# The opening of a fused attention and expert kernel, written out operation by operation

## The chip, the cores and the metric

The kernel runs on one core of one Trainium2 chip. The metric is the device time of one launch, in microseconds (us), as the median over several runs. Before the change it is 823.41 us (three runs, 822.85 to 825.19).

## The reference, cut to what matters

Attention over a band of keys for 4 batches, 8 heads, 576 positions and 64 dimensions, and then a mixture of four experts for every one of the 2304 positions:

```
scores = q @ k.T / sqrt(64)             # heads 0-3: the last 32 keys
scores = where(mask, scores, -1e9)      # heads 4-7: every 4th of the last 128 keys
attn   = exp(scores - max) / (sum + 1e-9)
x      = attn @ v                       # 2304 x 512 after a transpose of the heads
p      = domain_probs / (sum + 1e-9)
out    = sum over e of p[:, e] * (relu(x @ w1[e]) @ w2[e])   # w1[e] 512 x 1024, w2[e] 1024 x 512
```

All data are float32. The products of the experts are made from a high and a low part of each operand, three matmuls each, in a scheme with fewer block products (the names B11, B21, T1, S1 and so on are blocks and sums of blocks).

## The kernel before, in words

**Attention in steps.** A group is two heads of one batch and 192 positions; a step (`steps[m]`) is two groups. Each step goes through the same operations: `s_qk` (24 small matmuls on TensorE into two PSUM banks, tile `sc`, L300), `s_max` (six VectorE instructions that add the mask and take the row's extreme value, tiles `sm` and `nm`, L314), `s_sub` (GpSimd, L328), `s_exp` (ScalarE, L335), `s_sum` (VectorE: a sum, an added epsilon and a reciprocal, L345 to L351), `s_norm` (GpSimd, L358), `s_tr` (three transposes on TensorE into `pt`, L369, and ScalarE's copy into `pts`, L373), `s_av` (24 small matmuls into two banks `po`, L389) and `s_out` (two copies from `po` into the rows of x, tile `xr`, by ScalarE, L413, or VectorE, L411). The tiles `sc`, `pt` and `po` share a ring of four PSUM banks.

**Rounds.** The loop at L921 goes through rounds n = 0, 1, 2 and so on. In each it emits, in the order of a table (`first`, `ahead`, `turned`, `apart`, L419 ff.), the operations of several steps: the scores of step n, the sums of step n-1, the transposes of step n-2 and the product with v of step n-3. Between rounds `dummies` (L820, tile `wt`) put matmuls without use on TensorE. What one engine executes is then in exactly the order in which the program wrote it; engines wait for each other by semaphores.

**From attention to experts.** Steps 0 to 4 give the first 384 rows of x that the first expert product needs: block B11 from steps 0 to 2, block B21 from steps 3 and 4. `START` is 7, the round after which these are done. `x_part` splits a block into a high part (`xh_B`, ScalarE, L130) and a low part (`xl_B`, VectorE for one half and GpSimd for the other, L127); `w1_split` does the same with w1 (tiles `g1h`, `g1l`, and `hh12`, `hl12` for block A21), `w2_late` with w2 (`w2h`, `w2l`). `experts` emits the products: `m1x` and `m1y` (L475), then `m` (L579), whose results VectorE adds into `acc` (L583, L588). From then on attention steps are woven between expert products.

**Loads.** SyncE (queue SP) issues almost every load, in the order of the list `loads` (L879); ScalarE issues k of step 0 and the masks. A load goes out when its condition in `ready` holds, and an item that is not ready holds back what follows. v of a step is two transfers, one to partitions 0 to 63 and one to partitions 64 to 127. The entry `fenced` puts a one-element memset on VectorE ahead of v of steps 2, 3 and 4, and w1 has one too (L108), so that these transfers leave after VectorE has reached that place. w1 of the first unit comes in halves: A11 and A21 first (`("w1", 0)`), A12 and A22 later (`("rest", 0)`). The eight hardware semaphores of the transfers are used in turn, so a transfer also waits until the one eight places before it has landed.

## Time and profile before

| | us |
|---|---|
| median of three runs | 823.41 (822.85 to 825.19) |
| the profiled execution | 823.21 |
| its span, first to last instruction | 821.4 |
| TensorE matmuls busy | 812.7 (99%) |
| VectorE / ScalarE / GpSimd busy | 483.5 (59%) / 314.7 (38%) / 390.3 (48%) |
| first expert product m1x starts | 23.49 |
| its second operand block, from steps 3 and 4 | 27.03 |
| the expert products m (L579) go on after their last wait in the opening | 34.27 |
| granted TensorE clock, mean | 1.00 |

Times in the trace count from the first instruction of the span. The busy share of TensorE is a sum over matmul records and counts dummies as work; what a stretch is limited by is read from the chain of waits, which goes back from the last instruction to what released each step.

### The profile page before, as it was taken

To read this page: it belongs to the slowest core of one execution; us is meant where nothing else is said; L and a number is where in the kernel's file an instruction comes from. 1 tells how busy PE (TensorE), PEld (TensorE's weight loads), DVE (VectorE), ACT (ScalarE), POOL (GpSimd) and SP (SyncE) were. 2 spreads that over 40 slices of the span, in tenths; PEclk is the share of its full clock that TensorE was granted. 3 is DMA by queue.
4 is the path that set the end of the run, shared out by engine and by line. 5 is a ranking of instruction groups with operands and counts; after the bars stand their busy time and mean duration, and the time that the engine had idled before them with its cause. 6 is when DMAs were issued, how large, how long until landed. Compare 5 with 4: busy or idle time off the path is not lost.

```text
span 821.4 us, 15447 instructions
## 1 busy us (share of the span) xinstructions
PE 812.7 (99%) x6162; PEld 720.8 (88%) x6162; DVE 483.5 (59%) x1058; ACT 314.7 (38%) x749; POOL 390.3 (48%) x465
## 2 busy tenths in 40 slices
PE   8999999999999999999999999999999999999998
PEld 5778888888888889889889889889889989989987
DVE  5887557665765777555554554554554554555555
ACT  3554454544455446224223323323323323333321
POOL 4546878786777879334233233233243143153110
PEclk9999999999999999999999999999999999999999
DMA  7764624245211124110010010010010010010003
GB/s 230 230 180 132 193 71 133 83 128 158 91 53 52 52 92 140 35 43 26 26 51 27 26 52 26 26 52 26 27 52 26 26 52 26 27 51 1 1 26 128
DMA packets 46770, 59.15 MB, mean 72 GB/s; under 512 B 2905, under 2 KB 36313, under 8 KB 46699
## 3 DMA queue, kind: packets, MB, share of 16 engines
q1 hardware_dynamic: 46283, 57.75, 22.4%
q8 instruction: 48, 0.79, 0.4%
q10 hardware_dynamic: 416, 0.43, 0.1%
q14 instruction: 23, 0.19, 0.1%
HBM read 53.45 MB, written 4.72 MB: 71 GB/s over the span
## 4 chain that ended last, share of the span: by engine, by line
PE 92%; DVE 4%; DMA 1%; ACT 1%; issue 1%; POOL 0%; SPq 0%; POOLq 0%; DVEq 0%; ACTq 0%
PE m L579 46%; PE m1y L475 24%; PE m1x L475 18%; PE po L389 2%; DMA r<-w 1%; PE sc L300 1%; PE wt L824 1%; PE pt L369 1%; DVE xr L227 1%; DVE acc L588 1%; DVE sm L314 1%; DVE hl L499 0%; DVE su L345 0%; ACT hh L493 0%; DVE su L347 0%
## 5 line engine op out<-in xcount | busy, mean ns | idle before, releaser
L588 DVE SCALAR_TENSOR_TENSOR acc<-m,pn,acc 128x512 f32<-128x512 f32 (+1 forms) x271 | 202.2, 747 | 132.0 <-PE m L579 131.9
L579 PE MATMUL m<-w2h,hh 128*128 128x512 f32 x578 | 227.7, 394 | 0.8 <-DVE acc L588 0.3
L579 PE MATMUL m<-w2l,hh 128*128 128x512 f32 x578 | 225.5, 390 | 0.0
L127 POOL TENSOR_TENSOR g2l<-r,g2h 128x256 fp32r<-128x256 f32 x116 | 85.2, 759 | 235.0 <-PE m L579 212.7
L579 PE MATMUL m<-w2h,hl 128*128 128x512 f32 x578 | 179.0, 390 | 0.0
L493 ACT ACTIVATE hh<-s 128x384 fp32r<-128x384 f32 x92 | 48.3, 526 | 236.3 <-DVE s L516 185.2
L579 PEld LDWEIGHTS m<-w2h,hl 128*128 128x128 f32 x578 | 108.3, 188 | 24.5 <-DVE hl L499 1.0
L579 PEld LDWEIGHTS m<-w2h,hh 128*128 128x128 f32 x578 | 108.5, 188 | 23.2 <-DVE acc L588 2.6
L579 PEld LDWEIGHTS m<-w2l,hh 128*128 128x128 f32 x578 | 108.6, 188 | 19.5
L127 POOL TENSOR_TENSOR g1l<-r,g1h 128x256 fp32r<-128x256 f32 x93 | 70.0, 773 | 65.6 <-ACT g1h L130 65.6
L127 POOL TENSOR_TENSOR w2l<-r,w2h 128x512 fp32r<-128x512 f32 x58 | 75.2, 1315 | 47.1 <-ACT w2h L130 47.1
L535 DVE TENSOR_TENSOR s<-m1y,s 128x384 f32<-128x384 f32 x46 | 25.6, 556 | 93.8 <-PE m1y L475 92.3
L526 ACT ACTIVATE u<-m1y 128x384 f32<-128x384 f32 x46 | 22.6, 492 | 146.0 <-PE m1y L475 146.0
L499 DVE SCALAR_TENSOR_TENSOR hl<-s,hh 128x384 fp32r<-128x384 f32 x92 | 55.3, 601 | 27.7 <-ACT hh L493 27.5
L475 PE MATMUL m1y<-xh_T,g2h 128*128 128x384 f32 x152 | 51.9, 341 | 0.0
L475 PE MATMUL m1y<-xl_T,g2h 128*128 128x384 f32 x152 | 51.2, 337 | 0.0
L475 PE MATMUL m1y<-xh_T,g2l 128*128 128x384 f32 x152 | 51.0, 336 | 0.0
L130 ACT ACTIVATE g2h<-r 128x256 fp32r<-128x256 f32 x120 | 42.2, 407 | 0.8 <-POOL r L168 0.8
L475 PE MATMUL m1x<-xh_B,g2h 128*128 128x384 f32 x124 | 41.7, 337 | 0.0
L475 PE MATMUL m1x<-xl_B,g2h 128*128 128x384 f32 x124 | 41.7, 336 | 0.0
L475 PE MATMUL m1x<-xh_B,g2l 128*128 128x384 f32 x124 | 41.4, 334 | 0.0
L130 ACT ACTIVATE w2h<-r 128x512 fp32r<-128x512 f32 x64 | 38.3, 622 | 4.6 <-DMA r<-w 4.6
(133 smaller groups left out, 1477.2 us busy)
## 6 DMA issues: line engine op xcount, KB each, us to landing
r<-w SPq DMA_DIRECT2D x63, 512.0 KB, 3.3
v_s<-vw SPq DMA_DIRECT2D x48, 192.0 KB, 4.6
k_s<-kT SPq DMA_DIRECT2D x23, 224.0 KB, 4.8
q_s<-qT SPq DMA_DIRECT2D x24, 192.0 KB, 4.7
out<-acc SPq DMA_DIRECT2D x17, 256.0 KB, 2.0
r<-w SPq DMA_DIRECT2D x2, 256.0 KB, 4.3
out<-acc SPq DMA_DIRECT2D x2, 128.0 KB, 1.9
k_s<-kT ACTq DMA_DIRECT2D x1, 224.0 KB, 3.7
```

What stands on the lines that cost most here:

```text
L127: lo_eng.tensor_tensor(out=lo, in0=src, in1=hi.bitcast(F32), op=ALU.subtract)
L130: nc.scalar.activation(out=hi, in_=src, func=AF.Copy)
L227: nc.vector.tensor_tensor(out=quarter(i, d), in0=quarter(i, a), in1=quarter(i, b), op=ALU.subtract)
L300: nc.tensor.matmul(banks[swap][o:o + QB, i * KB:(i + 1) * KB], q_s[h, c0:c0 + QB], k_s[h, c0:c0 + KB], start=True, stop=True, skip_group_c ...
L389: nc.tensor.matmul(po[k][64 * j:64 * j + 64, o:o + QB], v_s[rows, j, 2 * i + half, :], ts_[rows, c:c + QB], start=True, stop=True,)
L475: nc.tensor.matmul(bank, w[:, k], x[:, k], start=(first and k == 0 and i == 0), stop=(last and k == 1 and i == 2), skip_group_check=True,)
L493: nc.scalar.activation(out=hi, in_=src, func=AF.Relu)
L499: nc.vector.scalar_tensor_tensor(out=lo, in0=src, scalar=0.0, in1=hi.bitcast(F32), op0=ALU.max, op1=ALU.subtract)
L526: nc.scalar.activation(out=u2, in_=x, func=AF.Copy)
L535: nc.vector.tensor_tensor(out=s5, in0=x, in1=s5, op=ALU.add)
L579: nc.tensor.matmul(po, h, w[:, d], start=(n == 0 and x == 0), stop=(n == 3))
L588: nc.vector.scalar_tensor_tensor(out=acc[:, d], in0=po, scalar=pn[:, tt, e:e + 1], in1=acc[:, d], op0=ALU.mult, op1=ALU.add,)
```

## The change

The rounds 0 to 7 no longer follow one table. `opening` lists the operations of every round. In it the sums of step n-2 (before: n-1) stand inside the maxima of step n: `s_both` emits the sum, then three of the six maxima, then the epsilon and the other three, then the reciprocal. The product with v of step m comes in round m+4 (before: m+3), and the scores of step 3 come ahead of the first transpose. Steps 3 and 4 get softmax buffers of their own, in tiles that the experts use later (`s1`, `hh21`). The second half of v of steps 0 to 3 is issued by ScalarE at the start, the first half by SyncE; the fences of v of steps 2 to 4 and of w1 go, and the first half of w1 goes out in round 1, ahead of v of step 1. The high parts of A11 and A21 are made in round 3, their low parts held until round 6. The copies out of `po` for steps 2, 3 and 4 are shared, one by ScalarE and one by VectorE (before: both by VectorE for steps 1 and 2, both by ScalarE for the others). Five dummies instead of seven stand between the rounds (1792 columns instead of 2560). After round 7 the program is as before.

```diff
-            if u in (0, 2):
+            if u == 2:
                 nc.vector.memset(raw1[u][:, 0, :1], 0.0)
...
-        def load_v(n, gs, fence):
-            t = ap.tile([128, 2, GB, 64], F32, tag="v", name="v_s", bufs=VB)
+        def load_v(n, gs, fence, halves=range(2), queue=nc.sync):
+            if n not in v_of:
+                v_of[n] = ap.tile([128, 2, GB, 64], F32, tag="v", name="v_s", bufs=VB)
+            t = v_of[n]
             if fence:
                 nc.vector.memset(t[:, 0, 0, :1], 0.0)
-            for k, (b, p, gi) in enumerate(gs):
-                nc.sync.dma_start(
+            for k in halves:
+                b, p, gi = gs[k]
+                queue.dma_start(
                     out=t[KB * k:KB * (k + 1)], in_=vw[b, p][:, :, gi * GB:(gi + 1) * GB, :]
                 )
-            v_of[n] = t
 
         def s_qk(n, gs):
             banks = [pa.tile([128, 512], F32, tag="pa", name="sc") for _ in gs]
...
-        def s_max(n, gs):
+        def max_parts(n, gs):
             banks = st[n]
-            sm = ap.tile([128, 2 * GS, KB], F32, tag="sm", name="sm", bufs=3)
+            if n in (3, 4):
+                sm = fp.tile([128, TH], F32, tag=("s1", "hh21")[n - 3], name="sm")
+                sm = sm.rearrange("q (k c) -> q k c", c=KB)
+            else:
+                sm = ap.tile([128, 2 * GS, KB], F32, tag="sm", name="sm", bufs=3)
             nm = ap.tile([128, 2 * GS], F32, tag="nm", name="nm", bufs=3)
...
-            st[n] = (sm, nm)
+                st[n] = (sm, nm)
+                yield
+
+        def s_max(n, gs):
+            for _ in max_parts(n, gs):
+                pass
 
         def s_sub(n, gs):
             sm, nm = st[n]
...
+            next(beside, 0)
             for su, rc, sm in ops:
                 nc.vector.tensor_tensor(
                     out=su, in0=su, in1=eps.to_broadcast([128, 2 * GS]), op=ALU.add
                 )
+            for _ in beside:
+                pass
             for su, rc, sm in ops:
                 nc.vector.reciprocal(out=rc, in_=su)
 
         def s_sum(n, gs):
             s_sums([(n, gs)])
+
+        def s_both(n, gs):
+
+            s_sums([(n - 2, steps[n - 2])], max_parts(n, gs))
 
         def s_norm(n, gs):
             sm, rc = st[n]
...
-                if 0 < n < 3:
+                if 1 < n < 5 and k:
...
-        ahead = (
-            (s_qk, 0), (s_max, 0), (s_sum, 1), (s_sub, 0), (s_norm, 1), (s_exp, 0),
-            (s_av, 3), (s_tr, 2),
+        stages = (first, apart, then)
+        opening = (
+            ((s_qk, 0), (s_max, 0), (s_sub, 0), (s_exp, 0)),
+            ((s_qk, 1), (s_max, 1), (s_sub, 1), (s_exp, 1)),
+            ((s_qk, 2), (s_both, 2), (s_sub, 2), (s_norm, 0), (s_exp, 2)),
+            ((s_qk, 3), (s_both, 3), (s_sub, 3), (s_norm, 1), (s_tr, 0), (s_exp, 3)),
+            ((s_qk, 4), (s_both, 4), (s_sub, 4), (s_norm, 2), (s_av, 0), (s_tr, 1), (s_exp, 4)),
+            ((s_sum, 3), (s_norm, 3), (s_av, 1), (s_tr, 2)),
+            ((s_sum, 4), (None, 0), (s_norm, 4), (s_tr, 3), (s_av, 2), (s_tr, 4)),
+            ((s_av, 3), (s_av, 4)),
         )
-        turned = ((s_tr, 2), (s_av, 3))
-        stages = (first, apart, then, ahead, turned)
 
         def pairs_of_steps(new, old, begun, loaded):
 
...
         qk_done, av_done = [0], [0]
         shares = []
         ready = {"w2": lambda u: u < 1 or (u - 1, 1) in w2_op and (u < 2 or n >= OPEN)}
-        ready["w1"] = lambda u: n >= (needed[0] + 1, 0, OPEN)[u]
+        ready["w1"] = lambda u: n >= (1, 0, OPEN)[u]
         waits = {
-            needed[0] + 1: needed[0] + 1, needed[1] + 1: OPEN - 2, needed[1] + 2: OPEN,
+            needed[0] + 1: START - 1, needed[1] + 1: OPEN - 2, needed[1] + 2: OPEN,
         }
         ready["qk"] = lambda m: m < qk_done[0] + QKB and n >= waits.get(min(m, needed[1] + 2), 0)
-        fenced = {2: (3, 0), 3: (3, 1), 4: (3, 1), 7: (START + 4, 0), 8: (START + 5, 0)}
+        fenced = {7: (START + 4, 0), 8: (START + 5, 0)}
         ready["v"] = lambda m: (
             m < av_done[0] + VB
             and (m <= needed[1] or m <= qk_done[0] and n >= OPEN)
-            and (n, mid) >= fenced.get(m, (0, 0))
+            and (n, 0) >= fenced.get(m, (0, 0))
         )
 
         def load(what, m):
             if what == "qk":
                 load_qk(steps[m], nc.sync if m else nc.scalar, m in waits)
             elif what == "v":
-                load_v(m, steps[m], m in fenced)
+                load_v(m, steps[m], m in fenced, range(1 if m < VB else 2))
+            elif what == "half":
+                load_v(m, steps[m], False, range(1, 2), nc.scalar)
             elif what == "masks":
                 load_masks()
             elif what == "rest":
...
-            ("qk", 0), ("masks", 0), ("qk", 1), ("qk", 2), ("v", 0), ("qk", 3), ("qk", 4),
-            ("v", 1), ("v", 2), ("v", 3), ("v", 4), ("w1", 0), ("qk", 5), ("rest", 0), ("probs", 0),
+            ("qk", 0), ("masks", 0), ("half", 0), ("half", 1), ("half", 2), ("half", 3),
+            ("qk", 1), ("qk", 2), ("v", 0), ("qk", 3), ("qk", 4), ("w1", 0), ("v", 1), ("v", 2),
+            ("v", 3), ("v", 4), ("rest", 0), ("qk", 5), ("probs", 0),
             ("w2", 0), ("qk", 6), ("w1", 1), ("qk", 7), ("v", 5), ("qk", 8), ("qk", 9),
...
-                flush()
-                holding.clear()
                 due = 0
-            early_order = {4: 3, 5: 3, START - 1: 4}.get(n, START + 1 < n < OPEN - 2)
-            for k, order in enumerate((stages[early_order], stages[2])):
+                if not 3 < n < START:
+                    flush()
+                    holding.clear()
+            if n <= START:
+                for stage, m in opening[n]:
+                    if stage is None:
+                        flush()
+                        holding.clear()
+                        continue
+                    stage(m, steps[m])
+                    av_done[0] += stage == s_av
+            for k, order in enumerate((stages[START + 1 < n < OPEN - 2], stages[2])):
+                if n <= START:
+                    continue
                 for stage, after in order:
                     m = step_at.get(n - after, -1)
                     if m >= 0 and k == (m > needed[1]):
...
-                dummies(*((384,), (384,), (384,), (), (384,), (), (128,))[n])
-                step()
-                if n > 4:
+                if n < 5:
+                    dummies(384 if n < 4 else 256)
+                if n in (3, START - 1):
                     step()
                     step()
                 continue
```

TensorE, from the scores of step 2 on, before (`wt` dummies, `sc` scores, `pt` transposes, `po` products with v):

```order
L300 MATMUL sc<-k_s,q_s 32x64 x24
L824 MATMUL wt<-ident 128x512
L824 MATMUL wt<-ident 128x384
L369 MATMUL pt<-ident,sm 128x128 x3
L824 MATMUL wt<-ident 128x384
L300 MATMUL sc<-k_s,q_s 32x64 x24
L389 MATMUL po<-pts,v_s 64x32 x24
L369 MATMUL pt<-ident,sm 128x128 x3
L300 MATMUL sc<-k_s,q_s 32x64 x24
L389 MATMUL po<-pts,v_s 64x32 x24
L369 MATMUL pt<-ident,sm 128x128 x3
L824 MATMUL wt<-ident 128x384
```

TensorE at the same place, after:

```order
L302 MATMUL sc<-k_s,q_s 32x64 x24
L848 MATMUL wt<-ident 128x384
L302 MATMUL sc<-k_s,q_s 32x64 x24
L388 MATMUL pt<-ident,sm 128x128 x3
L848 MATMUL wt<-ident 128x384
L302 MATMUL sc<-k_s,q_s 32x64 x24
L408 MATMUL po<-pts,v_s 64x32 x24
L388 MATMUL pt<-ident,sm 128x128 x3
L848 MATMUL wt<-ident 128x256
L408 MATMUL po<-pts,v_s 64x32 x24
L388 MATMUL pt<-ident,sm 128x128 x6
L408 MATMUL po<-pts,v_s 64x32 x24
```

The scores of step 3 now stand ahead of the first transposes, and only one dummy is left ahead of them; behind the scores of step 4 follow five products with v instead of four.

SyncE's queue, from the loads of step 2 to the first half of w1, before (v_s_115 is v of step 0, q_s_156 q of step 3):

```order
L275 DMA q_s_111<-qT 128x384
L276 DMA k_s_112<-kT 128x2x224
L285 DMA v_s_115<-vw 64x2x384 x2
L275 DMA q_s_156<-qT 128x2x192
L276 DMA k_s_157<-kT 128x2x224
L275 DMA q_s_204<-qT 128x2x192
L276 DMA k_s_205<-kT 128x2x224
L285 DMA v_s_208<-vw 64x2x384 x2
L285 DMA v_s_265<-vw 64x2x384 x2
L285 DMA v_s_338<-vw 64x2x384 x2
L285 DMA v_s_342<-vw 64x2x384 x2
L111 DMA r1_432<-w1 128x2x256
```

SyncE's queue at the same place, after (v_s_107 is v of step 0, q_s_162 q of step 3, r1_208 w1):

```order
L275 DMA q_s_119<-qT 128x384
L276 DMA k_s_120<-kT 128x2x224
L288 DMA v_s_107<-vw 64x2x384
L275 DMA q_s_162<-qT 128x2x192
L276 DMA k_s_163<-kT 128x2x224
L275 DMA q_s_204<-qT 128x2x192
L276 DMA k_s_205<-kT 128x2x224
L111 DMA r1_208<-w1 128x2x256
L288 DMA v_s_109<-vw 64x2x384
```

Ahead of q of step 3 one half of v is left, and w1 stands ahead of v of step 1.

ScalarE at the start, before:

```order
L276 DMA k_s_103<-kT 128x2x224
L416 DMA mask_95<-masks 128x384
L335 ACT_TABLE_LOAD
L335 ACTIVATE sm_144<-sm_144 128x384
L335 ACTIVATE sm_186<-sm_186 128x384
```

ScalarE at the start, after:

```order
L276 DMA k_s_103<-kT 128x2x224
L435 DMA mask_95<-masks 128x384
L288 DMA v_s_107<-vw 64x2x384
L288 DMA v_s_109<-vw 64x2x384
L288 DMA v_s_111<-vw 64x2x384
L288 DMA v_s_113<-vw 64x2x384
L346 ACT_TABLE_LOAD
L346 ACTIVATE sm_150<-sm_150 128x384
L346 ACTIVATE sm_192<-sm_192 128x384
```

Four half transfers of v now stand ahead of the table load and of the first exponential.

## Rows read from the trace of the kernel before

**Rows 1.** Page, parts 1, 3 and 4: busy time; a DMA queue; the chain by engine.
```profile
PE 812.7 (99%) x6162; PEld 720.8 (88%) x6162; DVE 483.5 (59%) x1058; ACT 314.7 (38%) x749; POOL 390.3 (48%) x465
...
q8 instruction: 48, 0.79, 0.4%
...
PE 92%; DVE 4%; DMA 1%; ACT 1%; issue 1%; POOL 0%; SPq 0%; POOLq 0%; DVEq 0%; ACTq 0%
```

**Rows 2.** Chain of waits, 0 to 50 us: start, duration, what ran or was waited for.
```profile
19.03 5.02 DMA r<-w
...
25.79 0.34 DVE xl_B L127
...
27.18 0.60 DVE w2l L127
...
34.27 1.68 PE m L579 x6
```

**Rows 3.** Timeline of PE: start, duration, line, operation, count, idle before and its releaser.
```profile
11.02 0.81 PE L824 MATMUL wt<-ident 128*128 128x384 f32 x2
11.76 0.72 PE L300 MATMUL sc<-k_s,q_s 64*32 64x64 f32 x48
12.41 0.90 PE L389 MATMUL po<-pts,v_s 64*64 64x32 f32 x48
13.26 0.53 PE L369 MATMUL pt<-ident,sm 128*128 128x128 f32 x3
13.72 0.72 PE L300 MATMUL sc<-k_s,q_s 64*32 64x64 f32 x48
14.38 0.92 PE L389 MATMUL po<-pts,v_s 64*64 64x32 f32 x35
16.53 0.42 PE L389 MATMUL po<-pts,v_s 64*64 64x32 f32 x13 [1.23 <-issue]
...
22.54 1.01 PE L389 MATMUL po<-pts,v_s 64*64 64x32 f32 x46 [0.70 <-issue]
23.49 0.45 PE L475 MATMUL m1x<-xh_B,g1h 128*128 128x384 f32 x1
```

**Rows 4.** Timelines of SP's queue and of ScalarE, first 8 us, same columns.
```profile
2.66 0.43 SPq L276 DMA_DIRECT2D k_s<-kT  x1
3.14 1.80 SPq L285 DMA_DIRECT2D v_s<-vw  x2
...
1.74 1.28 ACT L335 ACT_TABLE_LOAD   x1 [1.74 <-issue]
7.90 0.52 ACT L335 ACTIVATE sm<-sm 128x384 f32<-128x384 f32 x1 [4.88 <-POOL sm L328]
```

**Rows 5.** DMA issues with median us to landing; landing of k_s, then v_s, to 36 us.
```profile
k_s<-kT ACTq DMA_DIRECT2D x1, 224.0 KB, 3.7
...
DMA to landing us min/median/max: 3.5/4.4/5.6
...
DMA to landing us min/median/max: 3.3/4.5/7.0
```

**Rows 6.** Windows: stretch, busy per engine, PE clock, DMA share, GB/s.
```profile
3.00:7.00 4.00, 4.00 (x86) 1.98 (x86) 0.96 (x12) 0.02 (x1) 0.00 (x0) 1.00 1.08 384
7.00:9.00 2.00, 2.00 (x99) 1.27 (x75) 1.50 (x13) 0.52 (x1) 1.30 (x2) 1.00 1.09 271
```

**Rows 7.** Groups by line, 0 to 34 us: count, busy us, mean ns, idle before.
```profile
L373 ACT ACTIVATE pts<-pt 128x384 f32<-128x384 f32 x5 | 2.4, 489 | 3.2 <-PE pt L369 3.2
L127 DVE TENSOR_TENSOR xl_B<-xr,xh_B 128x384 fp32r<-128x384 f32 x2 | 2.1, 1052 | 2.2 <-ACT xh_B L130 2.2
...
L130 ACT ACTIVATE xh_B<-xr 128x384 fp32r<-128x384 f32 x4 | 1.9, 519 | 0.0
...
L411 DVE COPY xr<-po 128x192 f32<-128x192 f32 x4 | 1.2, 353 | 0.5 <-PE po L389 0.5
...
L283 DVE MEMSET v_s<- 128x1 f32 x3 | 0.1, 59 | 0.0
```

More of the change, by code (lines that the diff above doesn't have):

```diff
@@ L335, in s_exp, with s_sums @@
             nc.scalar.activation(out=st[n], in_=st[n], func=AF.Exp, scale=-1.0)
-        def s_sums(of):
+        def s_sums(of, beside=()):
+            beside = iter(beside)
             ops = []
@@ L466, in pairs_of_steps @@
                 yield
-        return chunk, load_masks, load_qk, load_v, stages, pairs_of_steps
+        return chunk, load_masks, load_qk, load_v, stages, pairs_of_steps, opening
     def product(bank, u, a, m, b_, first, last=True):
@@ L718 @@
         steps = []
-        pools["chunk"], load_masks, load_qk, load_v, stages, turn = attention(
+        pools["chunk"], load_masks, load_qk, load_v, stages, turn, opening = attention(
             ap, xr_pool, pa, steps
@@ L840 @@
         for n, i, names in (
-            (done(*plains[0]), 0, ("B11",)), (done(*plains[0]), 1, ("B11",)),
+            (START - 1, 0, ("B11",)), (START - 1, 1, ("B11",)),
             (START, 0, ("B21",)), (START, 1, ("B21",)),
@@ L921 @@
         for n in range(at(len(steps) - 1) + 2):
-            mid = 0
             load_ready()
@@ L942 @@
                             continue
-                        if n == 2 and stage == s_tr:
-                            dummies(512, 384)
                         stage(m, steps[m])
-                        if n == 3 and stage == s_max:
-                            mid = 1
-                            load_ready()
                         av_done[0] += stage == s_av
@@ L959 @@
             first_x.clear()
-            if n == 6:
+            if n == 3:
+                holding.add(n)
                 prepare(w1_split, 0)
```

## Prediction

> **What bounds the kernel now.** I read the page's busy times and its chain by engine first. TensorE is busy 99% of the span and makes up 92% of the chain [rows 1], so from the moment at which the expert products run without a gap, nothing on another engine matters. The chain of waits over the first 50 us says when that moment comes: w1's second half lands, ScalarE and VectorE split x and w1, and VectorE reaches `w2l` at 27.18; from there a fixed run of VectorE work leads to 34.27, where TensorE goes on with `m` [rows 2]. The program after `m1x` is the same in both kernels, so I measure the change at one point: **when does VectorE start `w2l`** (27.18 before)? What is won or lost there I carry to the end one for one.
>
> Then TensorE's timeline backwards from `m1x`. The scores of step 4 start at 13.72 and `po` of step 4 ends at 23.49: 9.77 us. In that stretch two products stand still with nothing to wait for in the program: `po` of step 1 breaks off and goes on at 16.53 after 1.23 us, `po` of step 4 at 22.54 after 0.70, both "issue" [rows 3]. The engine has 6162 matmuls and as many weight loads, and the instruction queue carried 48 packets [rows 1]: 12324/48 = 257 instructions in a packet. Between the two stalls 124 matmuls and 124 loads run, 248 and their waits, which fits one packet. I read the stalls as TensorE out of instructions. The stalled products are late by more than the idle time: 14.38 to about 16.88 and about 21.54 to 23.49, together 4.45 us where two undisturbed ones take 2 x 0.85 (12.41 to 13.26), so 2.75 in all.
>
> **The opening of the loads.** After the change SP's queue holds one half of v ahead of q and k of step 3 instead of two, which saves half of the 1.80 us of issue [rows 4]. But a load also waits for the one eight places before it, and ScalarE's four halves take places. k of step 2 now waits for k of step 0, issued at 0.73 with 3.7 us to landing [rows 5], so it leaves at about 4.4 instead of 2.66 [rows 4]. With 0.43 for it, 0.9 for the half of v and the next place, held by a load that lands near 6.5, k of step 3 leaves at about 7.0.
>
> When does it land? A transfer of k takes 3.5 to 5.6 us, median 4.4 [rows 5]: 10.5 to 12.6. By bytes: up to it 2816 KB are asked for, 960 of them v, where before 384 KB of v were. At the 384 GB/s of 3 to 7 us all would be in by 3.0 + 7.5 = 10.5; but between 7 and 9 us, with v's halves in flight, only 271 GB/s move at the same busy share, 1.09 against 1.08 [rows 6], and at that rate after 7.0 it is 12.0. I take 5.2 us, nearer to the largest, as so much stands ahead: **scores of step 3 at 12.3**, against 11.76 [rows 3]. The Trainium skill ("DMA: Bandwidth & Descriptors", "Rules for kernel authors") says that two transfers to disjoint partition halves share the same 16 engines and gain nothing by being apart. By it the halves on two queues are only more bytes ahead, and the sum has 12.0 for 12.3; this trace agrees, with its 271 GB/s at a full busy share.
>
> The new order puts the scores of step 3 ahead of the first transposes, so what delays k of step 3 now delays `pt` and `po` too. Behind it come `sc` 0.65, `pt` 0.46 and a dummy of 0.74 to 0.84 [rows 3]: scores of step 4 at **14.3** (13.72 before). Bounds: 12.5 with a landing after 3.5 us, 14.6 after 5.6, 16.0 after the 7.0 that a v transfer once took [rows 5].
>
> **From the scores of step 4 to the last po.** Before: 9.77 - 2.75 = 7.02 without the stalls. The change adds a product, `po` of step 0, 0.85 (12.41 to 13.26), and a transpose of step 1, 0.46 (13.26 to 13.72), and drops 256 columns of dummies, 0.49 at the rate of 384 in 0.74 (11.02 to 11.76) [rows 3]: 7.84. The count of instructions up to the two places hardly changes, so the packets still end in `po` of steps 1 and 4. TensorE comes to the first about 3.0 us after 14.3, at 17.3, later than 16.53, when that packet was there before: no stall. It would come to the second at about 21.4, and before that packet was there at 22.54: a stall of 1.1. Bounds for the stalls: 0 to 2.75. With 1.1 the last `po` ends at 14.3 + 8.9 = 23.2 (23.49 before).
>
> **From the last po to w2l.** Before: 27.18 - 23.49 = 3.69, of which a part waits for w1's second half, issued 19.03 and 5.02 in landing [rows 2]. After, SP issues it about 16.6 to 17, as the fences and four half transfers are gone from SP; it lands near 22 and nobody waits. Two paths remain.
> - Through `po`: copy 0.35, split 0.52 (one bank each, the copies now shared between two engines) [rows 7], and 1.39 from `xl_B` to `w2l` [rows 2], with 0.5 for the second bank and handovers: 2.8, so 26.0.
> - Through `pt` of step 4, two products ahead of the end: ScalarE's `pts` 0.49 stands ahead of the split of B11, 2 x 0.52 less overlap, 0.93; VectorE's `xl_B` 1.05 stands ahead of its two copies 0.70; then 0.52 [rows 7] and 1.39: 5.1. `pt` of step 4 ends 5.8 after the scores of step 4 (`sc` 0.65, three `po` 2.55, four `pt` 2.1, a dummy 0.49) plus a stall where it lies ahead. 14.3 + 5.8 + 1.1 + 5.1 = 26.3.
>
> I take the later, **w2l at 26.3, 0.9 earlier**. The profiled execution took 823.21 with a span of 821.4, so 822.3; the median shown, 823.41, lies 0.2 above that execution, and I forecast **822.4**.
>
> **Edits at nothing.** Four memsets of 0.06 less on VectorE [rows 7], which waits for the scores there anyway. ScalarE's four issues, two of which wait for earlier landings (about 6.3), and then the table load 1.28: done about 7.6, and the first exponential needed 7.90 [rows 4]. The cover is 0.3 us; when it is gone every later step shifts by the excess, but the wait for k of step 3 covers this for another 0.5. New softmax buffers free steps 3 and 4 from older ones; TensorE's order keeps them from starting earlier. Sums inside the maxima: one VectorE order against another with the same instructions; norm of step 0 moves behind the subtraction of step 2, and this ends ahead of 12.95, when `pt` can start at the earliest.
>
> **Rivals.**
> - *Slower: v's halves hold back k of step 3.* At a landing of 7.0 [rows 5] the scores of step 4 start at 16.0 and `w2l` at 28.0: 824.0; when the next packet also counts from the later start, up to 0.9 more. I take 824.4. It decides once `sc` of step 3 starts after 13.2, where 0.9 are used up. For it: 960 KB of v ahead of k and 271 GB/s. Against it: the landing of 7.0 is an extreme and k's own largest is 5.6. Chance 0.22.
> - *No difference: the instruction packets set the pace.* Between the stalls lie 16.53 to 22.54, 6.0 us; if the second packet comes 6.0 after the first place is passed, at 23.3, the stall is 1.9, `po` ends near 24.2 and `w2l` starts at 27.0 to 27.2: 823.2. For it: two stalls with nothing to wait for; against: 4.1 us (12.41 to 16.53) were enough for the packet before. Chance 0.15.
> - *Faster: k lands in its median and no stall is left.* Landing 4.4, `sc` of step 3 at 11.4, of step 4 at 13.4, `w2l` at 26.3 - 0.9 - 1.1 = 24.3 at best; w1's split and w2 hold it some: 820.3 to 822.0, I take 821.2. For it: issue of SP saved, one product and its queue ahead. Chance 0.23. The Trainium skill ("Runtime: NRT & Kernel Launch", "Instruction fetch mechanics") has blocks of 256 instructions whose crossing is mostly hidden; by it the stalls are not fetches, or end, and this rival holds, with 1.1 off the sum. The trace agrees with the 256 (257 in a packet), not with hidden: 1.23 + 0.70 us idle.
>
> **How the numbers follow.** Forecast 0.40, with its own range 821.4 to 823.8 (scores of step 4 between 13.4 and 14.6, one stall more or less). Eight in ten: from inside the faster rival, 820.7, to inside the slower, 824.9. A measurement tells 0.3%, 2.5 us: faster than 820.9 needs the good end of the faster rival, 0.14 with surprises; slower than 825.9 needs the late landing and both stalls together, 0.11; 0.75 between.
>
> **What would show it.** Right: k of step 3 issued near 7.0, `sc` of step 3 between 11.8 and 12.6 with a wait on the DMA ahead of it; `sc` of step 4 at 14.3; no "issue" idle in `po` of step 1 and about 1 us in `po` of step 4; w1's second half landed before 23; `w2l` at 26.3. Wrong: `exp` of step 0 after 7.9 (ScalarE's queue), `pt` waiting for GpSimd rather than for `sc`, or a tail from `sc` of step 4 to the last `po` unlike 8.9. If `w2l` moves and the end does not follow, the premise of a fixed path from 27.18 falls.

## The result and the profile after

The changed kernel takes 828.05 us (median of 12 runs, 824.94 to 831.37) against 823.63 for the kernel before in the same comparison (12 runs, 821.98 to 827.13): a ratio of 1.0052, 95% interval 1.0031 to 1.0073. It is slower by about 4.3 us, and the forecast was 822.4. The profiled execution took 826.73, with a span of 824.9. The twelve executions lie in two groups of six, 824.94 to 826.73 and 829.37 to 831.37, and the profile is of the first, so that what follows accounts for 3.5 us of span and not for the second group.

The chain's shares by engine, first of before [rows 1] and now of after: TensorE has 89% instead of 92%, waits for DMA have 4% instead of 1%.

```profile
PE 89%; DVE 4%; DMA 4%; ACT 1%; issue 1%; SPq 0%; POOL 0%; ACTq 0%; DVEq 0%; POOLq 0%
```

TensorE's timeline of after in the opening, which answers to [rows 3]:

```profile
9.62 0.81 PE L302 MATMUL sc<-k_s,q_s 64*32 64x64 f32 x48 [0.94 <-DMA k_s<-kT]
10.36 0.91 PE L848 MATMUL wt<-ident 128*128 128x384 f32 x2
14.18 1.05 PE L302 MATMUL sc<-k_s,q_s 64*32 64x64 f32 x48 [2.90 <-DMA k_s<-kT]
15.16 0.90 PE L388 MATMUL pt<-ident,sm 128*128 128x128 f32 x3
15.85 1.48 PE L848 MATMUL wt<-ident 128*128 128x384 f32 x2
17.27 0.97 PE L302 MATMUL sc<-k_s,q_s 64*32 64x64 f32 x48
...
20.71 0.90 PE L408 MATMUL po<-pts,v_s 64*64 64x32 f32 x48
...
24.09 1.71 PE L408 MATMUL po<-pts,v_s 64*64 64x32 f32 x96
25.73 0.44 PE L499 MATMUL m1x<-xh_B,g1h 128*128 128x384 f32 x1
```

TensorE waits for k twice, 0.94 us ahead of the scores of step 2 and 2.90 ahead of those of step 3. The scores of step 4 start at 17.27 instead of 13.72. Both stalls without a releaser are gone in this execution: `po` of step 1 (20.71) and of steps 3 and 4 (24.09) run through. `m1x` starts at 25.73, 2.24 us later than before.

The windows of after (columns as in [rows 6]) show a second part of the loss. From 11 to 20 us the granted clock is 0.78, 0.50 and 0.59, where the whole execution of before had a mean of 1.00; 0.50 is the lower of the two levels, 1.2 GHz. The dummy of 384 columns that took 0.81 before takes 1.48 at 15.85.

```profile
7.00:9.00 2.00, 1.68 (x51) 0.86 (x50) 1.45 (x19) 1.34 (x2) 0.95 (x2) 1.00 1.10 273
9.00:11.00 2.00, 1.38 (x50) 0.97 (x50) 0.93 (x9) 0.52 (x1) 0.71 (x1) 1.00 1.08 231
11.00:14.00 3.00, 0.27 (x1) 0.00 (x0) 0.99 (x9) 0.52 (x1) 1.61 (x2) 0.78 1.09 366
14.00:17.00 3.00, 2.82 (x53) 1.87 (x53) 1.56 (x15) 0.49 (x1) 0.55 (x1) 0.50 0.76 157
17.00:20.00 3.00, 3.00 (x101) 2.52 (x101) 1.35 (x15) 1.44 (x5) 1.22 (x3) 0.59 0.06 17
```

The queues of SyncE and ScalarE in after, which answer to [rows 4], and the landing of k_s, to [rows 5]:

```profile
4.31 0.37 SPq L276 DMA_DIRECT2D k_s<-kT  x1
4.72 0.65 SPq L288 DMA_DIRECT2D v_s<-vw  x1
6.40 0.39 SPq L275 DMA_DIRECT2D q_s<-qT  x1
7.50 0.37 SPq L276 DMA_DIRECT2D k_s<-kT  x1
...
10.31 10.61 SPq L288 DMA_DIRECT2D v_s<-vw  x5
20.97 0.59 SPq L111 DMA_DIRECT2D r<-w  x1
```
```profile
1.76 4.74 ACTq L288 DMA_DIRECT2D v_s<-vw  x4
6.53 1.28 ACT L346 ACT_TABLE_LOAD   x1 [6.53 <-issue]
8.25 0.52 ACT L346 ACTIVATE sm<-sm 128x384 f32<-128x384 f32 x1 [0.44 <-POOL sm L339]
```
```profile
DMA to landing us min/median/max: 3.6/6.1/8.4
```

k of step 3 leaves at 7.50 and, by the chain of waits of after, takes 6.54 us. Not only what stood ahead of it held it back: the loads asked for up to it are 2816 KB, 2.88 MB, and by its landing at 14.04 3.70 MB had moved, so 0.8 MB of loads issued behind it moved before it was complete. The view of DMA of after, from 0 to 14.04 us:

```profile
DMA packets 3657, 3.70 MB, mean 263 GB/s; under 512 B 270, under 2 KB 3656, under 8 KB 3656
```

SyncE then sits on v of step 4, which waits until 19.74 for the buffer that `po` of step 0 (18.17 to 19.58) reads, so w1's second half leaves at 20.97 instead of 19.03, w2 at 23.93 instead of 20.03. That decides the end of the opening:

```profile
7.50 6.54 DMA k_s<-kT
...
23.93 5.20 DMA r<-w
...
29.82 0.69 DVE w2l L127
```

`w2l` starts at 29.82, 2.64 later than before. The span is 3.5 longer; the rest is about what the later waits of `m` and `pt` cost, of which before had only that for `acc`, with 0.3:

```profile
PE sc L302 <- DMA k_s<-kT: 3.8, 2, 2.9
...
PE m L603 <- DVE acc L612: 0.6, 1, 0.6
...
PE pt L388 <- DVE nm L320: 0.4, 1, 0.4
PE m L603 <- DVE hl L523: 0.4, 1, 0.4
```

### The profile page after: what moved, and what is told of

The parts are those of the page before. It is cut to its first block, busy times and chain, and to the rows that moved or that the text cites. A ratio compares the mean times of both kernels' runs of the same rounds, so it can differ in the third digit from the quotient of the medians.

```text
span 824.9 us, 15433 instructions
## 1 busy us (share of the span) xinstructions
PE 812.5 (98%) x6158; PEld 721.1 (87%) x6158; DVE 484.1 (59%) x1053; ACT 315.6 (38%) x750; POOL 388.6 (47%) x465
## 4 chain that ended last, share of the span: by engine, by line
PE 89%; DVE 4%; DMA 4%; ACT 1%; issue 1%; SPq 0%; POOL 0%; ACTq 0%; DVEq 0%; POOLq 0%
PE m L603 45%; PE m1y L499 23%; PE m1x L499 17%; DMA r<-w 2%; PE po L408 1%; PE sc L302 1%; DMA k_s<-kT 1%; DVE xr L227 1%; DVE sm L320 1%; PE pt L388 1%; DMA v_s<-vw 1%; DVE acc L612 1%; DVE hl L523 1%; DVE w2l L127 0%; ACT w2h L130 0%
```

## The experiments

All ratios are to the kernel before, run beside each experiment, with 95% intervals. The first theory was that v's halves hold k back and that nothing else is wrong.

**e1: v whole on SyncE.**
```
-("half", 0), ("half", 1), ("half", 2), ("half", 3),
-load_v(m, steps[m], m in fenced, range(1 if m < VB else 2))
+load_v(m, steps[m], m in fenced, range(2))
```


> The changed kernel, but every half of v is issued by SyncE at the place where the first half stood; ScalarE issues none of v. The order of the operations, the missing fences and the early w1 stay. Theory (the three further halves of v ahead of k of steps 2 and 3 hold TensorE up, and its clock falls in the wait): k of step 2 is issued near 2.7 us and k of step 3 near 6.5, the scores of step 2 wait for nothing, those of step 3 less than 0.5 us, the granted clock is 1.00 from 11 to 20 us, the scores of step 4 start before 14.5 and the time is 821.0 to 823.5, ratio to before 0.997 to 1.000. Rival (the new order of the operations costs the time, whatever the loads): scores of step 4 still after 16, ratio 1.004 to 1.006.

Measured 826.68 us, ratio 1.0043 (1.0031 to 1.0056). The waits for k shrink to 0.47 ahead of the scores of step 3 and 0.41 ahead of those of step 4, which start at 13.24, as the theory had it, but the time hardly moves. In their place TensorE stalls with no releaser. Timeline and windows of e1:

```profile
18.10 0.47 PE L408 MATMUL po<-pts,v_s 64*64 64x32 f32 x15 [0.93 <-issue]
...
25.91 1.49 PE L408 MATMUL po<-pts,v_s 64*64 64x32 f32 x44 [1.79 <-issue]
```
```profile
17.00:20.00 3.00, 2.08 (x32) 1.54 (x24) 2.43 (x5) 1.17 (x4) 1.99 (x3) 0.73 0.77 225
20.00:24.00 4.00, 4.00 (x104) 3.55 (x103) 0.43 (x2) 2.18 (x6) 0.44 (x1) 0.50 0.96 272
24.00:28.00 4.00, 2.21 (x50) 2.06 (x47) 1.59 (x3) 1.00 (x3) 0.55 (x1) 0.50 1.04 337
28.00:34.00 6.00, 6.00 (x71) 5.44 (x70) 3.97 (x18) 2.21 (x6) 1.53 (x2) 0.67 0.30 63
```
The clock falls behind the first stall. What that costs is read from e1's own chain, the six `m1x` products at the low level and later at the full one:
```profile
27.40 2.22 PE m1x L499 x6
...
32.89 1.24 PE m1x L499 x6
...
41.37 1.06 PE m1x L499 x6
```

**e2: halves of steps 0 and 1 only.**
```
-("half", 0), ("half", 1), ("half", 2), ("half", 3),
+("half", 0), ("half", 1),
-range(1 if m < VB else 2)
+range(1 if m < 2 else 2)
```

> The changed kernel, but only the second halves of v of steps 0 and 1 go out by ScalarE at the start; steps 2 and 3 are loaded whole by SyncE at their old place. Theory (bytes ahead of k): 384 KB fewer stand ahead of k of step 3, 1.4 us at 271 GB/s, so its wait is 1.0 to 1.8 us instead of 2.9, the scores of step 4 start 1.4 to 2 us earlier than 17.27, and the ratio to before is 1.001 to 1.003, half way. Rival (the order): unchanged, ratio 1.004 to 1.006, waits elsewhere on TensorE.

Measured 828.94, ratio 1.0068 (1.0056 to 1.0080). The waits for k fall by 1.1 in all (to 1.08 and 1.67, where 1.0 to 1.8 was expected for the second), and the scores of step 4 start at 16.35, 0.92 earlier where 1.4 to 2 was expected; but `po` of step 4 then stalls 3.33 us. The theory's ratio misses; the rival had waits elsewhere on TensorE, though not so large a ratio.
```profile
27.36 1.49 PE L408 MATMUL po<-pts,v_s 64*64 64x32 f32 x44 [3.33 <-issue]
```

**e3: only the new loading of v, in the kernel before.** `load_v` is that of the change; the fences stay, on the half that SyncE loads.
```
-("qk", 0), ("masks", 0), ("qk", 1), ("qk", 2),
+("qk", 0), ("masks", 0), ("half", 0), ("half", 1), ("half", 2), ("half", 3),
+("qk", 1), ("qk", 2),
```

> The kernel before with only the new loading of v: second halves of steps 0 to 3 by ScalarE at the start, first halves by SyncE at the old places; fences, order of operations and w1 as before. Theory (bytes ahead of k): the scores of step 2 and 3 wait for k as in the changed kernel, together 3 us or more, the clock falls behind the wait, ratio to before 1.003 to 1.007. Rival (the order): TensorE has transposes to do before the scores of step 3 here, the waits are under 1 us, ratio 0.999 to 1.001.

Measured 825.99, ratio 1.0033 (1.0019 to 1.0046). TensorE waits 1.12 ahead of the scores of step 2 (the row names VectorE, but k of step 2 lands at 9.46 and the scores start at 9.71) and 1.18 for k of step 3, 2.3 in all against none before, where the theory had 3 or more. The splitting of v alone costs 2.7 us. k of step 3 lands at 14.23 here, as late as in the changed kernel, with w1 at its old place: the early w1 is not what delays it.

**e4: dummies in the places of the wait.**
```
+                if n in (1, 2):
+                    dummies(*((512,), (512, 512, 512))[n - 1])
```


> The changed kernel with dummies in the two places where TensorE waits for k: one more of 512 columns ahead of the scores of step 2, three more ahead of those of step 3, some 2.6 us of work without use. The loads are the same. Theory (a part of the loss is the clock granted after the wait): clock 1.00 from 11 to 20 us, scores of step 3 as late as before (near 14.2), scores of step 4 near 16.2 instead of 17.27, time 1 to 2 us below the changed kernel, ratio to before 1.002 to 1.004. Rival (the clock costs nothing because the next waits absorb it): the time of the changed kernel, ratio 1.005.

Measured 829.98, ratio 1.0070 (1.0048 to 1.0092). The clock does stay at 1.00 from 11 to 20 us and the scores of step 4 start at 16.97. With TensorE at full clock, `po` of step 4 runs dry instead (a row of e4's timeline), and the clock falls there, to 0.78 from 24 to 28 us and 0.58 from 28 to 34. Neither reading had a time above that of the changed kernel (the intervals of the two overlap).
```profile
26.92 1.62 PE L408 MATMUL po<-pts,v_s 64*64 64x32 f32 x47 [2.27 <-issue]
```
So e1, e2 and e4 each shorten one wait and get the other. The second set asks what the stall is.

**e5: short dummies in the kernel before.**
```
-            for c in cols:
+            for c in [128] * (sum(cols) // 128):
```

> The kernel before, with each dummy cut into pieces of 128 columns: the same columns of work, but 17 more matmuls and as many weight loads ahead of po of step 1 (34 records), 19 and 38 ahead of po of step 4. Loads, waits and all other engines are the same. Theory (the idle 'issue' stretches on TensorE are waits for a packet of instructions, so their place follows the count of instructions): the first stall moves from 35 of 48 records of po of step 1 to its beginning (0 to 5 of 48), the second from 2 of 48 of po of step 4 into po of step 3, at 10 to 18 of 48. Rival (the stall is a wait for data or a buffer of that product, which the records don't show): the stalls stay at 35 of po of step 1 and 2 of po of step 4.

One run, 826.58. The first stall moves to behind 3 of 48 records of `po` of step 1 (0 to 5 expected, 35 before), with the same products, loads and waits: its place follows the count of instructions. The clock fell to 0.50 behind it, and at this pace the second, expected in `po` of step 3, did not come.
```profile
16.30 1.01 PE L389 MATMUL po<-pts,v_s 64*64 64x32 f32 x45 [1.28 <-issue]
```

**e6: as e1, w1's second half and what follows held back** by a memset on VectorE, issued in round 6.
```
+        elif u == 0:
+            nc.vector.memset(raw1[u][:, 2, :1], 0.0)
...
+        ready["rest"] = lambda u: "rest" in gate
...
+                        gate.add("rest")
+                        load_ready()
```

> As e1 (all of v issued by SyncE), and the second half of w1, with everything behind it on SyncE's queue, waits for a memset that VectorE reaches at about 19.7 us; in e1 it was issued at 17.15. Theory (the packet of instructions that TensorE needs in po of step 4 stands in the DMA engines behind the loads issued between 17 and 20 us, e1's stall of 1.79 us ended at 25.91 and the clock fell to 0.50 behind it): the queues are near empty when it is asked for, TensorE has no 'issue' idle over 0.3 us in po of step 4, the clock stays over 0.9 from 20 to 28 us, and the time is 821.0 to 823.0, 4 to 5 us under e1. Rival (the packet comes late whatever the loads): stall and clock as in e1, and the time 826 to 828, or more, since w1 is later.

Measured 824.77, ratio 1.0011 (0.9992 to 1.0029): 0.3% under the ratio of e1, and no longer to be told from before. But the stall is there, 1.07 us instead of 1.79, with the clock at 0.66 behind it, though the queues were empty. The window of 19.75 to 20.25 us of e6 holds one packet, the instructions':
```profile
22.37 0.89 PE L410 MATMUL po<-pts,v_s 64*64 64x32 f32 x44 [1.07 <-issue]
```
```profile
DMA packets 1, 0.02 MB, mean 33 GB/s; under 512 B 0, under 2 KB 0, under 8 KB 0
...
q8 instruction: 1, 0.02, 12.2%
```
It starts at 19.94 with nothing ahead of it, and TensorE goes on 2.43 later. In before it starts at 20.32, 2.22 ahead of 22.54.

**e7: the new order with the old loads**, on top of e1.
```
+        fenced = {2: (3, 0), 3: (3, 1), 4: (3, 1), 7: (START + 4, 0), 8: (START + 5, 0)}
...
-("w1", 0), ("v", 1), ("v", 2), ("v", 3), ("v", 4),
+("v", 1), ("v", 2), ("v", 3), ("v", 4), ("w1", 0),
...
-            if n == 3:
-                holding.add(n)
+            if n == START - 1:
                 prepare(w1_split, 0)
```

> The new order of the operations (interleaved sums, po a round later, scores of step 3 first, two softmax buffers, fewer dummies, shared copies) with the loads of before: v whole on SyncE, fences on v of steps 2 to 4 and on w1, w1 behind v of step 4, split in round 6. Theory (the loads, not the order, make the loss, by delaying k and the instruction packets): k of step 3 and the scores as in e1 (scores of step 4 near 13.3), the second stall under 1.2 us as in the kernel before, the clock over 0.95 to 34 us, ratio to before 0.997 to 1.001. Rival (the order makes the loss: the two stalled places lie closer together in time, since less waits between them): second stall 1.5 us or more and the clock near 0.5 behind it, ratio 1.003 to 1.006.

Measured 830.74, ratio 1.0083 (1.0059 to 1.0106), the slowest of all. My expectation falls and the rival holds in kind, with a larger loss than it had: the new order with the old loads loses more than with the new ones. `po` of step 4 stands still for 4.09 us (the row names a load of k, on which this product does not depend). The packet starts at 24.42, 2.54 ahead of the second row, and 1.55 after TensorE had run dry at 22.87. Behind the stall `m1x` waits 1.51 more for `g1h`: w1 is split in round 6 here, on ScalarE behind the copies of the stalled product.
```profile
21.86 1.01 PE L408 MATMUL po<-pts,v_s 64*64 64x32 f32 x52
26.96 1.50 PE L408 MATMUL po<-pts,v_s 64*64 64x32 f32 x44 [4.09 <-DMA k_s<-kT]
```

**e8: the kernel before without its fences** on v of steps 2 to 4 and w1.
```
-            if u in (0, 2):
+            if u == 2:
...
-        fenced = {2: (3, 0), 3: (3, 1), 4: (3, 1), 7: (START + 4, 0), 8: (START + 5, 0)}
+        fenced = {7: (START + 4, 0), 8: (START + 5, 0)}
```

> The kernel before without the fences on v of steps 2 to 4 and on the first half of w1: its transfers leave as soon as SyncE comes to them. Order of operations and of the queue unchanged. Theory (loads issued earlier stand ahead of the packet of instructions): the second half of w1 is issued 1.5 us or more before 19.03, the second stall grows from 0.70 us to 1.5 or more, the clock falls behind it, ratio to before 1.002 to 1.006. Rival (earlier loads only help, since w1's second half ended the wait ahead of the splits): ratio 0.998 to 1.000.

Measured 826.34, ratio 1.0023 (1.0004 to 1.0041). The second half of w1 left at 19.95, not earlier: q of step 5 stands ahead of it in SyncE's queue and waits 2.1 us for its own memset on VectorE (waits of SyncE's queue, 0 to 24 us):
```profile
SPq L275 <- DVE q_s L273: 2.1, 1, 2.1
```
It is the first stall that grows, from 1.23 to 2.08; the second falls to 0.16. The ratio is in the theory's range, but by the other stall. The profile is of a run with the clock at 1.00 (823.71); nine of the twelve had 0.994 or less and took 825.2 to 829.1.

**e9: two loads more in the kernel before.**
```
-("w1", 0), ("qk", 5), ("rest", 0),
+("w1", 0), ("extra", 0), ("extra", 1), ("qk", 5), ("rest", 0),
```

> The kernel before with two loads more on SyncE's queue, 192 KB each into a buffer that nothing reads, between the first half of w1 and q of step 5: 0.8 us of issue and about 1.4 us of transfer at 271 GB/s. Everything on TensorE is the same. Theory (the packet of instructions for po of step 4 waits behind the loads that stand in the queues between 17 and 20 us): the second stall grows from 0.70 us to 1.5 to 3 us, the clock falls behind it, ratio to before 1.002 to 1.006. Rival (the packet's delay is fixed and only the load of w1 is late): the stall stays under 1.2 us, w1's second half and with it w2l are 1.0 to 1.5 us later, ratio 1.001 to 1.002, clock 1.00.

Measured 824.89, ratio 1.0012 (0.9995 to 1.0029); the second stall is 0.98, the clock of the profile 1.00, and `w2l` starts at 28.24, 1.06 later. The rival's sizes are right, and the theory's stall of 1.5 to 3 us did not come. The test is a weak one: the share of the DMA engines from 17 to 20 us rose only from 0.82 to 0.85.

**e10 and e11: v of step 4 early**, in the tile that w1 of the second unit takes later; in e11 the pause stands behind w1's second half.
```
-            m < av_done[0] + VB
+            (m == 4 or m < av_done[0] + VB)
...
+                t = wp.tile([128, 4, FU], F32, tag="r1", name="v_s", bufs=2)
```

> As e6 (v on SyncE, second half of w1 and what follows held to about 19.7 us), and v of step 4 in a buffer of its own, so that it no longer waits for po of step 0 and leaves right behind v of step 3. The queues are then empty from about 17 to 19.7 us. Theory (the packet waits behind loads): no 'issue' stall in po of step 4 over 0.4 us (1.07 in e6), clock 0.99 or more to 34 us, time 820.5 to 822.5, ratio to before 0.996 to 0.999. The first stall may grow from 0.15 us, since v of step 4 now stands ahead of that packet. Rival (the time between packets is fixed): the second stall as in e6, about 1 us, ratio 1.000 to 1.002.

> As e10, but the second half of w1 leaves right behind v of step 4, ahead of the pause, and only what follows it on SyncE's queue is held to about 19.7 us. Theory: w1's second half lands before 20 us, 4 us earlier than in e10, but 256 KB more stand in the queues when the packet for po of step 4 is asked for, so its stall is between those of e10 and e1 (0.5 to 1.5 us); ratio to before 0.997 to 1.001. Rival (w1's landing decides, not the stall): under e10 by 1 us or more, ratio 0.995 to 0.997.

Measured 826.01, ratio 1.0025 (1.0008 to 1.0043), and 825.97, 1.0014 (0.9995 to 1.0032). In both the first stall grows, to 1.55 and 1.52, and the clock falls to 0.50 to 0.54 from 20 to 28 us; at that pace the second stall is 0.41 and none. The second theory is not refuted by this: e10's expectation had the first stall grow because v of step 4 now stands ahead of its packet, and that packet starts at 16.00 and 16.02 instead of 14.79 in e6. In e8, where v also leaves earlier, it starts at 15.23 instead of 14.01 in before. The second stalls of e10 and e11, at the low clock, say nothing of it.

The third theory: the packet goes with TensorE's own progress and takes 2.2 to 2.6 us from its start to the next matmul; a run of short products is used up sooner. The duration holds in every stall of these runs, with 2.20 (e14) to 2.84 (e11). (Counted from 9 us on, the second packet is the one that ends the first stall, the third the one that ends the second.)

**e12: as e6, two dummies ahead of po of step 4; e13: the kernel before, dummies ahead of po of steps 1 and 4; e14: of step 1 alone.**
```
+                    if stage == s_av and m == 4:
+                        dummies(512, 256)
```
```
+                        if stage == s_av and m in (1, 4):
+                            dummies(512, 384 if m == 1 else 128)
-                dummies(*((384,), (384,), (384,), (), (384,), (), (128,))[n])
+                dummies(*((384,), (384,), (384,), (), (384,), (), ())[n])
```


> As e6, with two dummies (512 and 256 columns, about 1.3 us, four matmul records) between po of step 3 and po of step 4, that is between the place at which the third packet started there (in the transposes of step 4) and the place at which TensorE ran out of instructions. Third theory (the packet starts at a place in TensorE's own instructions and takes 2.2 to 2.6 us until TensorE goes on, however empty the queues are; some 58 short matmuls then last only 1.0 to 1.4 us): the 'issue' idle in po of step 4 falls from 1.07 us to under 0.3, and as TensorE stays busy the clock stays over 0.98 from 20 to 34 us in the profile; time equal to or up to 1 us under e6, ratio to before 0.999 to 1.001. Rival (the packet comes by its own clock or behind loads): the stall keeps 0.8 us or more on top of the dummies, and the time is 1 us over e6 or more, ratio 1.002 or over.

> The kernel before, with dummies of 512 and 384 columns (about 1.6 us) ahead of po of step 1, where TensorE stalls 1.23 us, and one of 512 columns more ahead of po of step 4, where it stalls 0.70. Third theory, and that the clock falls after such stalls in a part of the executions (of 29 executions of before 14 had a mean clock under 0.998 and took 824.7 us or more): the stalls fall under 0.4 us each, the mean clock is 0.998 or more in at least 9 of 10 executions, median 822.3 to 823.5, ratio to before 0.998 to 0.9995. Rival (the dummies only add work and the clock falls for another reason): ratio 1.001 to 1.003, the mean clock spread as before.

> As e13, with the dummies ahead of po of step 1 alone, and the one of 128 columns ahead of po of step 4 as in the kernel before. Third theory: the first stall falls under 0.4 us, the second stays at 0.4 to 1.0; if it is the first, longer stall after which the clock falls, the times are those of e13 or 0.3 us less, else they spread as those of before. Rival: as for e13, 1.0005 to 1.002.

Measured 825.33, ratio 1.0015 (0.9999 to 1.0031); 824.48, 1.0009 (0.9996 to 1.0021); 824.50, 1.0009 (0.9998 to 1.0021). In e13 both products run through. Its timeline:
```profile
14.20 1.77 PE L824 MATMUL wt<-ident 128*128 128x512 f32 x4
15.90 0.90 PE L389 MATMUL po<-pts,v_s 64*64 64x32 f32 x48
...
20.97 1.35 PE L824 MATMUL wt<-ident 128*128 128x512 f32 x4
22.25 0.90 PE L389 MATMUL po<-pts,v_s 64*64 64x32 f32 x48
```
The packet for `po` of step 1 starts at 13.65 in e13 and 14.04 in e14, as in before (14.01), and the dummies last until it is there. Ten of e13's twelve executions have a mean clock of 1.000, against 13 of 29 of the kernel before beside it. In e14 the second stall is 1.43, above the 0.4 to 1.0 expected:
```profile
22.85 0.38 PE L824 MATMUL wt<-ident 128*128 128x128 f32 x2 [1.43 <-issue]
```
The third packet starts at 18.19 in e13 and at 20.65 in e14. Up to the end of `po` of step 3 both have the same instructions, and `po` of step 2 starts at 17.92 and 18.30, so TensorE's progress does not set this start. With a packet at 18.19 the second stall would have been gone without dummies too; what they do there is seen in e12 alone. In e12 `po` of step 4 runs through and the clock is 1.00 from 17 to 34 us (the fall behind k's wait, 1.83 here, stays); its third packet starts in the transposes of step 4, as in e6, at 20.99. That the dummies take the stall's place is thus shown for the first stall by e13 and e14 and for the second by e12, one profile each. The gain was not there: the end of the opening then waits for w1 and its splits (`w2l` at 28.27 in e13 for 27.18), and a dummy costs its own time. (Of the 29 executions that e13's expectation speaks of, 12 and not 14 had a clock under 0.998.)

The profiles fit what the second theory says of the start. In the new order the third packet starts in the transposes of step 4 in e6, e10, e11 and e12, where the share of the DMA engines from 20 to 24 us is 0.36 to 0.76. It starts later in e16 and e1, within `po` of step 3, and in e4, e2 and e7, 0.06, 0.89 and 1.55 us after TensorE had run dry; there the share is 0.87 to 0.96. (In the first two profiles of the changed kernel, with 0.67 and 0.59, the low clock came ahead of it, and it starts in the transposes of steps 2 and 3.) The row of e6, then that of e7 (columns as in [rows 6]):
```profile
20.00:24.00 4.00, 2.93 (x102) 2.64 (x102) 1.94 (x4) 2.44 (x7) 0.99 (x1) 0.91 0.62 170
20.00:24.00 4.00, 2.56 (x105) 2.10 (x103) 0.99 (x2) 2.65 (x7) 1.46 (x2) 0.94 0.89 255
```
So full queues go with a later start, and the 2.2 us or more from start to matmul come on top of it, with empty queues too. That the loads are what delays the start is not shown by an experiment of its own.

**e15 and e16: the changed kernel again.**

> The changed kernel as it is, profiled once more: its executions lie in two groups, 824.9 to 826.7 us and 829.4 to 831.4, and the profile shown is of the first. Theory (the second group has the wait for instructions too): an execution of 829 us or more shows the waits for k as in the first profile and besides 1.5 us or more of 'issue' idle in po of step 1 or 4, with the clock near 0.5 behind it. Rival (the second group only has a longer wait for k): no 'issue' idle over 0.5 us, k's wait 5 us or more.

> As e15, a third profile of the changed kernel, with the same two readings.

826.32 and 827.77. e15 is like the first profile: k's wait 3.24, the clock at 0.50, no stall. e16 has its wait for k in two parts, 1.74 ahead of the scores of step 3 and 1.50 ahead of those of step 4, the clock stays at 1.00 up to 24 us, TensorE is at full pace, and the stall comes, with a fall to 0.73 from 28 to 34 us:
```profile
26.02 0.89 PE L408 MATMUL po<-pts,v_s 64*64 64x32 f32 x43 [1.65 <-issue]
```
So the same kernel has either of the two. An execution of 829 or more was not caught in a profile, and neither reading of e15 was tested.

None of these is faster than the kernel before. e6, e9, e11, e12, e13 and e14 can't be told from it, and e6 has the lowest ratio of the forms of the new order, 0.4% under the changed kernel; the intervals of e11 and e12 overlap with its own. The parts of the new order (fewer dummies, the sums between the maxima, the softmax buffers, the shared copies) were not run apart from each other.

## Why the prediction was wrong

- **The scores of step 3 (12.3 forecast, 14.18 measured).** The issue was right in kind (k of step 2 at 4.31 for 4.4, k of step 3 at 7.50 for 7.0), the landing was not: 6.54 us for 5.2. This is the step that failed first. The landing kept its bound (7.0 at most), the scores of step 4 did not: 17.27 for 16.0 at most, as the clock came on top. I took the value near k's old landings, when 960 KB of v stood ahead of it. At the 271 GB/s of [rows 6] the bytes ahead gave 12.0, and from 9 to 11 us only 231 were moved; but counting the bytes ahead was itself too little, since 0.8 MB issued behind k moved before it landed. Of the rivals the slower one happened, with its place; it decided from 13.2 on. e3 and e1 show the halves from both sides: with them alone waits of 2.3 us in the old order, without them 0.9 in the new one. The new order waits for k by itself too, though: without halves e6, e10 and e12 wait 1.16, 1.31 and 1.83 ahead of the scores of step 3. And without halves e1 still has a ratio of 1.0043 of the 1.0052, so this rival names one cause of two.
- **Halves on two queues.** The Trainium skill ("DMA: Bandwidth & Descriptors", "Rules for kernel authors") has it that halves on two queues gain nothing. The trace agrees: 273 GB/s from 7 to 9 us with two queues at work, 271 before with one.
- **The clock was not in the sum at all.** The wait ahead of the scores of step 3 is followed by 0.50, in two of the three profiles of the changed kernel. The term missed is about 1.5 us in the first profile up to the end of the scores of step 4: from 14.18 to 18.17, 3.99 us, where the same four groups take 0.65 + 0.46 + 0.74 + 0.65 = 2.50 at the full level. My rival priced the wait at 824.4 without it.
- **The stalls.** That they are waits for instructions was right: e5 moves the place, and each stall of these runs ends 2.2 to 2.8 us after a packet starts. The value 1.1 would have been luck: 0 in two profiles of the changed kernel, 1.65 in the third, 0 to 4.09 in others of the new order. My reason, a packet that comes by the clock of the trace, fell: in the new order the third starts between 19.94 and 24.92. I took 256 columns of dummies out as a gain of 0.49; by e12 dummies ahead of `po` of step 4 cover the packet, but putting back just these was not tried.
- **w1's second half (16.6 to 17 forecast, 20.97 measured).** I left out that v of step 4 waits for `po` of step 0 and that SyncE waits with it. A later `po` thus holds w1 and w2, and `w2l` goes by w2 (landing 29.13), not by the two paths that I weighed.
- **The tail** from the scores of step 4 to the last `po` was right in size, 8.46 for 8.9, by luck: the stall of 1.1 did not come, and `po` of step 0 took 1.41 instead of 0.85 at the low clock. The premise that the end follows `w2l` one for one held for 2.64 of 3.5 us.
- **Edits at nothing.** ScalarE's table load ended at 7.81 for 7.6 and the first exponential came at 8.25 for 7.90, after 0.44 of waiting for GpSimd: the table was not what it waited for, as forecast. The sign of being wrong that I had set there (an `exp` of step 0 after 7.9) came, but not from the cause that I had named.
- **Two slips in the sums.** The path through `pt` adds the stall of 1.1, which by my own placing lies in `po` of step 4, behind that transpose; without it that path gives 25.2, and the later of the two is 26.0. And 822.3 with 0.2 more is 822.5. Both put right, the forecast is 822.2, no nearer to the result.

What stays open: what exactly starts a packet (TensorE stood in the transposes of step 4 when the third started in e6 and e10, in those of steps 2 and 3 in the changed kernel's first profile, and 2.5 us lie between e13 and e14), whether the loads are what delays it in e2, e4 and e7, and the slower half of the executions.

## What to carry to other kernels

Where short instructions run in long rows, a wait that you take away may be what gave the supply of instructions its time: look for idle time without a releaser, and price each wait also by the clock that is granted behind it. Before you put early loads ahead of others, add up the bytes that then stand ahead of the one that TensorE needs next, and those issued close behind it, and follow what each queue does behind an item that has to wait.

## What the runs showed of the hardware

- The place of a stall of TensorE follows the count of its instructions (e5), and dummies of few, long instructions take its place (e13 and e14 the first, e12 the second). From the start of the packet to the next matmul it takes 2.2 to 2.8 us.
- The granted clock fell to 0.50 behind an idle 2.90 us and behind stalls of 0.93 (e1) and 1.28 us (e5), but not behind 1.23 in the profile of before, 1.43 in e14 and 2.08 in e8, where it stays at 1.00: the length of one idle stretch does not decide it. Six `m1x` products take 2.22 us in e1 and e5 at the low level and 1.06 at the full one.
- The mean clock sorts the executions of the kernel before: of the 29 beside e12, the 20 fastest, up to 825.06 us, have 0.998 or more, and the seven slowest, from 825.49, have 0.996 or less.
